# Eleven VectorE units in 21 of 28 pairs, vertical results in tiles of 128 tokens, and fewer groups of projections, in a cross-window attention kernel

## The chip, the cores and the metric

The kernel runs on one core of one Trainium2 chip. The metric is the device time of one launch in microseconds (us), as the median of several runs. The core has a matrix engine (TensorE, PE in the profile; its weight loads are PEld), a vector engine (VectorE, DVE), an activation engine (ScalarE, ACT), a general one (GpSimd, POOL) and a queue for transfers (SyncE, SP).

## The reference

The input x is an image of 224 x 224 tokens with 96 channels, in bf16. The first 48 channels of q, k and v attend within horizontal stripes of 8 rows, the other 48 within vertical stripes of 8 columns. Each stripe holds 8 x 224 = 1792 tokens, and there are 28 of each kind.

```
qkv = einsum('bhwc,cd->bhwd', x, wqkv)
q, k, v = qkv[..., :C], qkv[..., C:2*C], qkv[..., 2*C:]
# horizontal: 28 stripes of 8 rows, channels 0..47
ah = softmax(einsum('bqc,bkc->bqk', qh, kh) * scale)
oh = einsum('bqk,bkc->bqc', ah, vh)
# vertical: 28 stripes of 8 columns, channels 48..95
av = softmax(einsum('bqc,bkc->bqk', qv, kv) * scale)
ov = einsum('bqk,bkc->bqc', av, vv)
return einsum('bhwc,cd->bhwd', concat(oh, ov), wo)
```

## The kernel before

**Pairs, chunks, units.** Two stripes make a pair P; pairs 0 to 13 are horizontal, 14 to 27 vertical. A pair's 1792 queries are cut into four chunks (512, 512, 512 and 256). For a full chunk a *unit* is one tile of 128 keys against 512 queries of both stripes; for the last chunk it is two tiles of keys against 256 queries. Either way a unit is a score tile of 128 x 1024 in two banks of PSUM, and a pair has 14 + 14 + 14 + 7 = 49 units, 1372 in all. Scores (`qk_op`, line 985) split the array of TensorE by rows, one stripe in each half; the product with the values (`pv_op`, line 938) splits it by columns, one stripe in each half. The code calls these two shapes of the array modes "q" and "v", and its planner charges a constant for a change between them.

**Two ways to the exponential.** Most units go through ScalarE (`add_a`, line 1007): one ACTIVATE with Exp from PSUM to `PT`, then one product with the values. The others go through VectorE (`add_d`): line 1045 turns scores into integers `I_sb`, lines 1058 and 1060 split off mantissa and exponent (`U_sb`, `E_sb`) for two units at a time, line 1064 multiplies `I_sb` and `U_sb` to `G_sb` (halves on GpSimd, or a whole unit on VectorE), and both `E_sb` and `G_sb` are multiplied with the values. `NDC` and `NDP` say how many units of each chunk go this way: `[4, 2, 2, 2]`, and `[4, 3, 2, 2]` in seven pairs. An odd unit at a pair's end is processed alone.

**Projections** (`prep`) for pair P + 1 are done beside the units of P, as small groups called fills: one matmul group into a bank and a copy out of it. There are four for k (line 689, copy 706, then its mean is subtracted), four for q (copy 700) and four for v (line 745, copy 750: 10 and 4 tiles of keys for each stripe).

**Outputs** (`fin`). When a chunk's values are summed, VectorE copies them to `OT_sb` (line 901), and groups of four tiles are multiplied with `wo`. One more column holds the sum of the softmax: a reciprocal (lines 778, 831) and a product (797, 835) normalize. A horizontal pair has 7 groups. Its result goes to a staging buffer, and 8 DMAs on SP's queue carry it into `Ph_sb`, laid out by image rows for the vertical pairs. A vertical pair has 8 groups (two stripes, four chunks of four tiles of 112 rows of the image, each tile two matmuls), GpSimd adds the part from `Ph_sb` (line 839), and 8 DMAs store it.

**Order.** The order of the operations on TensorE, VectorE and GpSimd is written out by hand in `PLAN`: one digit an operation, naming the stream that gives the next one (in "pe": 1 scores for ScalarE, 2 scores for VectorE, 3 and 4 products with the values, 5 output groups, 6 fills). `far` says which products of line 1064 go to GpSimd, `bank` which banks are used. Each engine runs its list in order. A small planner with fixed costs puts in the waits and orders SP's queue.

Of the kernel before, what the change touches and what calls it, by code (L numbers as in the profile page):

```python
# [25 lines left out]
NDP = {P: [4, 3, 2, 2] for P in range(3, 28, 4)}  # L26


def ndc(P, c):
# [5 lines left out]
        "00000000000000000066611216162164144116444216331641631264144126133136121464441144441243141461643143124143614124"  # L35
        "31431241641241641144533123414312414531631313631531544163124154312414316341261341146444145145416414361331251341"
        "24163114644441335154124163124163412144414412414441214461431231631231331261343114443311464454114644531541641544"
        "14613313461231541241631145444413123614411634541246134125414414123134123134414412613312316412314313412641341164"
        "46411344336154154441512441636141253143144163153164412415341241431443121434124144146123613414414616312513331214"
        "44144126133113643441164454164154415416313312631441251341441146346134123164124135411444461231341234144124135414"  # L40
        "41461361335124163154144416312351441216341146444145144613313461231541241631145444413316451541231641231644124144"
        "14412414431251331134443513412514312416441231331461641136446411634441451441533126144123614411634411336445124315"
        "41146431246144124143314124513412415411346431641354123164124134163312414612314412414411346441231631134644415416"
        "51441431233134113664412313412413414412414312316441134463123614412613412413541331464154113446415416415441541633"
        "13612351441241631145444133615415441261341231641241444133124144123154411344361361241354124144144126133113634641"
        "14544341431231641241644116345441511344633154114634512461341412461421414313412415431245141134433164124163412614"
        "41231431346154143146414614124142133136114634541144461153331146445315412461312416441241441331241431241544113443"
        "35124154136124416312413314616441231361412133413514516441261431144443113644616431241544123143144125144412413311"
        "36344144615412415312513331241641231431341164463614611463441244154124143134616411534461441136433412514441136445"
        "12316414441241331241441231531441436136123154124134133124614311544441146446413312316441261341146445314416313514"  # L50
        "46135124153164144412614412414413341241541231541344121334124163124164411344631634113444614514361331251441241634"
        "11464431146335144411634515412341641241464124131312414411335441241641233163124153124144133126414311644644131213"
        "34114644541641231644111354444316313124416341126441341412641441233144112335144116344461312351441231634143163414"
        "12531341461444133161544126134412613411544441146335411463451244161235144124164411442313154123514411464431641241"
        "45312416412416431431451311363444314614514531431261443126144411643314531146435124316412414612414531144214331451"
        "43143146312416412414531241431431261334111644433441331216441126341441164463111644335411164435421451436121544121"
        "44142164111343335124414412613312316412316413341216441341134446124611133544163124614431154444113634515441631231"
        "54124414314412614412416431313531441461241644123133126134124613411444531631143444416451441541431631236134123164"
        "11454441163354124163124513412414414412641441133354123414144126313312614412316413314641154344114464451461544154"
        "16313312613412541341146444136135412416312413514412461441444123135123154113644412463341124316441251341431341144"  # L60
        "44164615431631331216441451363125144411144463341645135154124163124614412514441441213341231541134446312163415414"
        "41334163123164412613412415441431441631231641236144115443411343634164125414312414314416416331541541544131253143"
        "12441641261441412441331261441243134133114644641331445144124164124164114643631416331531231631251441231644115444"
        "41245142131331164434124164125133144126133143314641164443113463351451544146123164412513411464441146335414412513"
        "41241641241644114344412513312415311464431241631431261341241634115444411433344164164154415414615416331231531231"
        "64114644441451241331631241634115444412415413312415331241441541341534125144124133133154412415312415431215441441"
        "2541431341143443114335513413541541541241544124144133141431344554344355"),
    "dve": (
        "00000000000000000333333332332344323332344332323442331234421232344332123344333331332344323323443333331323323441"
        "33333232344221442323212444433333333333333132332344133233332344231244423123244232333443133333332334432333331234"  # L70
        "42324421344233312344232344333333333331232344331323234433221442331333323443333233234433331323323443133333323234"
        "42212443313323324423333333144333323234431333233323442123324413333332344233232244132444333333321443324422124431"
        "32323443233344333333333331323323441333333323234422124433133234423233334413323233334433133333323234421233244133"
        "32324423333443332213344333331333332323442212443133323332442333444212333333324433331234423233244441333323132332"
        "44233333331243423333334431233333234424214423313323442323443333312323344333331333233323442123324412332324433444"
        "33333132332344333313333323234424214433213232344232333441233333234434331234423234421233443132334443233432344133"
        "33232344331333333232332443123323344313233234443233344433333132323443133333232324431234443313232344232344413323"
        "23334431333332333234423213444233123234423244433321333323443433333331234423232344443133232123244333344433333431"
        "32323443133332323442323144423312323442333443333333333312323344133332342334423123323344321323444234443333333142"
        "33332344313333333323234423123234431323344433233232344133232344434331323442333443333313233231244232444233444331"  # L80
        "33232334433133232332344332312344321323344423334443333331333232334433313233232444312332334431232323344344433333"
        "4333333123323413434323234434321332344321333323444323323323132334432444434343133333333233442441443433133333"),
    "pool": (
        "00000000022222122222222222222222222212222222222222222222212222222222222222222212222222222222222222221222222222"
        "22222222221222222222222222222222212222222222222222221222222222222222222221222222222222222222222212222222222222"
        "22222122222222222222222222222122222222222222222221222222222222222222212222222222222222212222222233332222223222"
        "21222232233222222223221222233222233333222222333221222232222333322222222332212232222333223222232221222322333222"
        "23222222321222333222232233222232212222223322333322223223322122333222233332222223222122233322322222233333222221"
        "2222222333222222332212222332233333222222223312222333332232233223332222333333333333333"),
    "far": (  # L90
        "11111111111111111111111111110111111111111111111111111111111111111111111111111011111111111111111111111111111111"
        "11111011111111111111110111111111111011111101111110111110101111111001111110110111111011101110111110101111011111"
        "1101110101011110111100111101101111110101111011110110011001110000000"),
    "bank": (
        "76547012376502064256045260426403640246024604602472026027062705205205204620462042540520752057302570264026406204"
# [274 lines left out]
FUSED = 0.45  # L370
PRIO = (1, 0, 3, 5, 4, 2)
DPRIO = (0, 1, 2, 3)
HALVES = False
LEAD, SPACE, PACE, FIRST = 8, 3, 0.9, 0


# [817 lines left out]
```

## Time and profile before

| | |
|---|---|
| median of 3 runs | 1016.58 us (1015.27 to 1017.64) |
| profiled execution, its own time | 1017.69 us |
| its span, first to last instruction | 1015.6 us |
| mean granted TensorE clock | 0.995 |
| ScalarE busy | 1000.0 us (98%) |
| VectorE busy | 925.3 us (91%) |
| GpSimd busy | 695.1 us (68%) |

A line of instruction groups gives source line, engine, operation, what it writes and reads, shapes and count, then busy time in us, mean ns of one, and the idle time of that engine just before such instructions with what ended it. Instructions that overlap their neighbours have a mean longer than their step.

### The profile page before, as it was taken

The numbers are of one execution on the slowest core, as the hardware profiler recorded it, in microseconds if no ns is written. First come the engines' busy times: TensorE is split into PE (matmuls) and PEld (weight loads), VectorE is DVE, ScalarE is ACT, GpSimd is POOL, SyncE is SP. The second block draws the span as 40 slices with busy tenths as digits, with TensorE's granted clock in tenths as the row PEclk, the third lists the DMA queues.
The fourth block names the chain that finished last, engine by engine and source line by source line (L and its number), as shares of the span: only waits on it lengthen the run. The fifth ranks groups of instructions, "written<-read, shape, count | busy, mean of one in ns | idle before, by whom it ended". The sixth has DMA issues, their size and how long they took to land.

```text
span 1015.6 us, 25611 instructions
## 1 busy us (share of the span) xinstructions
PE 1001.6 (99%) x10683; PEld 388.2 (38%) x10683; DVE 925.3 (91%) x1677; ACT 1000.0 (98%) x1094; POOL 695.1 (68%) x639
## 2 busy tenths in 40 slices
PE   8999999999999999999999999999999999999998
PEld 3333333443334334334333333433343343334333
DVE  7999988998989988999899899989998999999998
ACT  6999999999999999999999999999999999999997
POOL 2777577667666756666677777776777676777674
PEclk8999999999999999999999999999999999999999
DMA  5121323353524425232442112212122221222112
GB/s 108 38 29 37 66 28 56 46 65 29 65 38 39 53 39 65 28 44 42 49 60 49 30 37 60 42 39 48 39 44 42 59 44 38 56 42 39 25 26 52
DMA packets 189612, 46.61 MB, mean 46 GB/s; under 512 B 189384, under 2 KB 189384, under 8 KB 189496
## 3 DMA queue, kind: packets, MB, share of 16 engines
q1 hardware_dynamic: 188536, 44.49, 27.2%
q8 instruction: 83, 1.36, 0.6%
q10 hardware_dynamic: 960, 0.49, 0.2%
q14 instruction: 33, 0.27, 0.1%
HBM read 0.44 MB, written 9.63 MB: 10 GB/s over the span
## 4 chain that ended last, share of the span: by engine, by line
ACT 74%; PE 23%; DVE 2%; POOL 1%; issue 0%; DVEq 0%
ACT PT L1007 74%; PE ps L938 10%; PE ps L985 9%; PE ps L689 2%; PE ps L826 1%; DVE I_sb L1045 1%; PE ps L745 1%; POOL G_sb L1064 0%; PE ps L529 0%; DVE OT_sb L901 0%; DVE E_sb L1060 0%; DVE tmp L835 0%; DVE QT_sb L700 0%; DVE U_sb L1058 0%; DVE V_sb L750 0%
## 5 line engine op out<-in xcount | busy, mean ns | idle before, releaser
L1007 ACT ACTIVATE PT<-ps 128x1024 bf16<-128x1024 f32 x1085 | 996.0, 1134 | 4.5 <-PE ps L985 4.4
L1064 POOL TENSOR_TENSOR G_sb<-I_sb,U_sb 128x512 bf16<-128x512 bf16 x488 | 549.5, 1155 | 285.1 <-DVE E_sb L1060 259.2
L985 PE MATMUL ps<-QT_sb,KT_sb 48*128 48x512 bf16 (+1 forms) x3136 | 469.7, 357 | 6.1 <-ACT PT L1007 3.2
L1045 DVE TENSOR_SCALAR I_sb<-ps 128x1024 int16<-128x1024 f32 x287 | 350.4, 1221 | 29.8 <-PE ps L985 25.6
L938 PE MATMUL ps<-PT,V_sb 128*64 128x512 bf16 (+1 forms) x2450 | 373.7, 364 | 0.0
L985 PEld LDWEIGHTS ps<-QT_sb,KT_sb 48*128 48x128 bf16 x3136 | 125.2, 93 | 311.0 <-ACT PT L1007 235.7
L938 PEld LDWEIGHTS ps<-PT,V_sb 128*64 128x64 bf16 x2450 | 120.2, 109 | 122.1 <-issue 101.8
L938 PE MATMUL ps<-G_sb,V_sb 128*64 128x512 bf16 (+1 forms) x686 | 111.6, 354 | 0.0
L839 POOL TENSOR_TENSOR out_sb<-tmp,Ph_sb 112x384 bf16<-112x384 f32 x111 | 99.0, 915 | 13.6 <-DVE G_sb L1064 5.3
L938 PE MATMUL ps<-E_sb,V_sb 128*64 128x512 bf16 (+1 forms) x686 | 101.3, 353 | 0.5 <-DVE OT_sb L901 0.2
L1058 DVE TENSOR_SCALAR U_sb<-I_sb 128x2048 int16<-128x2048 int16 x147 | 101.2, 689 | 0.0
L1060 DVE TENSOR_SCALAR E_sb<-I_sb 128x2048 int16<-128x2048 int16 x147 | 99.0, 674 | 0.0
L689 PE MATMUL ps<-xT_sb,w_sb 96*64 96x512 bf16 (+1 forms) x444 | 83.0, 369 | 0.7 <-ACT xT_sb L655 0.4
L700 DVE TENSOR_SCALAR QT_sb<-ps 128x512 bf16<-128x512 f32 (+1 forms) x111 | 68.4, 619 | 15.6 <-PE ps L689 12.5
L901 DVE CAST OT_sb<-ps 128x512 bf16<-128x512 f32 x112 | 69.3, 619 | 4.1 <-PE ps L938 3.2
L706 DVE TENSOR_SCALAR_CACHE_REDUCE KT_sb<-ps 128x512 bf16<-128x512 f32 x110 | 67.2, 620 | 5.5 <-PE ps L689 5.2
L750 DVE CAST V_sb<-ps 128x480 bf16<-128x480 f32 (+1 forms) x112 | 55.7, 502 | 12.2 <-PE ps L745 11.3
L835 DVE TENSOR_TENSOR tmp<-ps,rc 112x384 f32<-112x384 f32 x111 | 61.6, 555 | 2.7
L718 POOL TENSOR_SCALAR KT_sb<-KT_sb,negmean 128x1792 bf16<-128x1792 bf16 x27 | 47.5, 1761 | 18.4 <-DVE E_sb L1060 14.8
L797 DVE TENSOR_TENSOR out_sb<-ps,rc 128x384 bf16<-128x384 f32 x98 | 54.5, 556 | 2.8
L938 PEld LDWEIGHTS ps<-G_sb,V_sb 128*64 128x64 bf16 x686 | 34.9, 108 | 39.6 <-issue 28.4
L938 PEld LDWEIGHTS ps<-E_sb,V_sb 128*64 128x64 bf16 x686 | 31.1, 108 | 34.9 <-issue 19.0
(44 smaller groups left out, 339.3 us busy)
## 6 DMA issues: line engine op xcount, KB each, us to landing
Ph_sb<-out_sb SPq DMA_DIRECT2D x112, 84.0 KB, 4.3
out_dram<-out_sb SPq DMA_DIRECT2D x111, 84.0 KB, 2.0
xT_sb<-in_x_dram SPq DMA_TRANSPOSE x251, 2.5
Ph_sb<-in_x_dram ACTq DMA_DIRECT2D x1, 336.0 KB, 3.2
out_dram<-out_sb ACTq DMA_DIRECT2D x1, 84.0 KB, 2.2
wo_sb<-in_wo_dram SPq DMA_DIRECT2D x4, 9.0 KB
wo_sb<-one_sb SPq DMA_DIRECT2D x4, 0.0 KB
w_sb<-in_wqkv_dram ACTq DMA_DIRECT2D x1, 54.0 KB, 5.0
```

Of the source, the lines that this page charges most:

```text
L689: ins = e.matmul(bk[64 * w:64 * w + 64, 0:qs], lhsT=w_sb[0:C, wblk(P, kind), :], rhs=rhs, start=True, stop=True)
L700: return e.tensor_scalar(dst, src, A128, None, ALU.mult)
L706: return e.tensor_scalar(dst, src, 1.0, None, ALU.mult, ALU.add, accum_out=acc)
L839: return e.tensor_tensor(out_sb[b][0:HB, :, w, 2 * c:2 * c + 2, :].rearrange("p h d c -> p d h c"), tmp[hold[1].tok["t"]][0:HB, 0:n, :].re ...
L901: return e.tensor_copy(OT_sb[b][:, q0:q0 + qs], bk[:, 0:qs])
L938: return e.matmul(bank(k.bank)[64 * w:64 * w + 64, x0:x1], lhsT=lhs(w, kts[i])[p0:p1], rhs=rhs(w, i, qs)[p0:p1, x0:x1], start=(op.tok["fir ...
L985: ins = e.matmul(bank(op.tok["s"][w])[:, i * qs:(i + 1) * qs], lhsT=KT_sb[b][64 * w:64 * w + C2, kt * 128:(kt + 1) * 128], rhs=QT_sb[b][64 ...
L1007: a.fn = lambda e: e.activation(PT[a.tok["p"]][:].rearrange("p (s n) -> p s n", s=2), two(q.tok["s"]), ACTF.Exp, scale=LN128)
L1045: return e.tensor_scalar(dst[:, at:at + 1024].rearrange("p (s n) -> p s n", s=2), two(src), 128.0 * ONE, 0.0, ALU.add, ALU.max)
L1058: f.fn = lambda e: e.tensor_scalar(U_sb[y()][:, 0:m], I_sb[y()][:, 0:m], M_FRAC, HALF, ALU.bitwise_and, ALU.bitwise_or)
L1060: x2.fn = lambda e: e.tensor_scalar(E_sb[x2.tok["l"]][:, 0:m], I_sb[y()][:, 0:m], M_EXP, E_LOW, ALU.bitwise_and, ALU.bitwise_or)
L1064: g.fn = lambda e: e.tensor_tensor(G_sb[x2.tok["l"]][:, i0:i1], I_sb[y()][:, i0:i1].bitcast(BF16), U_sb[y()][:, i0:i1].bitcast(BF16), ALU. ...
```

## The change

Units on VectorE become 3, 3, 3 and 2 by chunk in the 21 pairs whose number isn't 1 modulo 4; the other seven keep 4, 2, 2 and 2. Queries of vertical pairs are put in the order (row, column in the stripe), so that a tile of 128 tokens is 16 image rows by 8 columns, as the horizontal results already have it. Horizontal results are therefore written straight to `Ph_sb`, and the staging DMAs go. A vertical pair has 7 output groups in place of 8; those of the three full chunks take one stripe each, in full tiles of 128 tokens with the contraction in one half of the array's rows (`rowed`, mode "q"), and the last chunk does both stripes in one group. Stores of a vertical pair become 16, all issued when its seventh group is added; the last pair stores tile by tile. The last fills of k and q share one bank, and v takes groups of 10, 10 and 8 tiles over both stripes: 10 fills in place of 12. All lists of `PLAN` are new.

```diff
-NDP = {P: [4, 3, 2, 2] for P in range(3, 28, 4)}
+NDP = {P: [3, 3, 3, 2] for P in range(28) if P % 4 != 1}
...
-        Ph_sb = sb("Ph_sb", [128, 2, 2 * NPH, SW, C], BF16)
-        out_sb = [sb(f"out_sb{i}", [128, 2, 2, SW, C], BF16) for i in range(2)]
+        Ph_sb = sb("Ph_sb", [128, NPH, WB, C], BF16)
+        out_sb = [sb(f"out_sb{i}", [128, NKT, 2, C], BF16) for i in range(2)]
...
-                        if kind == "q" and is_h[P]:
+                        if kind == "q":
                             rhs = xT_sb[b][0:C, w, :].rearrange("c (g t) -> c g t", g=SW)[:, :, q0 // SW:(q0 + qs) // SW]
...
+                        else:
+                            dst = dst.rearrange("p (t d) -> p t d", d=SW)
+                            src = src.rearrange("p (d t) -> p t d", d=SW)
...
+                if kind == "k" and c == NCH - 1 and not startup:
+                    pe_q, ev_q = kq("q", c, part=True)
+                    pe_k = pe_fn
+                    pe_fn = lambda e, bk: (pe_k(e, bk[:, 0:qs]), pe_q(e, bk[:, qs:2 * qs]))[1]
+                    evs.insert(1, ("dve", 0.08 + qs / 960, lambda e, bk, op: ev_q(e, bk[:, qs:2 * qs], op), [], True, dve_ev, [], None))
...
-            def vv(w, k0):
-                n = min(VS, NKT - k0)
+            def vv(k0, n=None):
+                n = n or min(VS, 2 * NKT - k0)
...
-                work = [(kq, kind, c) for kind in "kq" for c in range(NCH)] + [(vv, w, k0) for w in range(2) for k0 in range(0, NKT, VS)]
+                work = [(kq, kind, c) for kind in "kq" for c in range(NCH - (kind == "q"))] + [(vv, k0) for k0 in range(0, 2 * NKT, VS)]
...
-                        return e.tensor_tensor(stage(b)[:, g[0]:g[0] + n, :], ...
+                        return e.tensor_tensor(Ph_sb[:, P, g[0]:g[0] + n, :], ...
...
-                            fn = lambda e, dw=dw: e.dma_start(Ph_sb[r0:r0 + 2 * SW, P // 7, :, dw, :], stage(b)[dw:128:8, :, :])
...
+                for ws in ((0,), (1,)) if nk == 4 else ((0, 1),):
+                    n = nk * len(ws)
+                    last = P == NP - 1 and c == NCH - 1
+                    rowed = VQ and len(ws) == 1
...
+                            if rowed:
+                                ins = e.matmul(bk3[:, s, :], lhsT=OT_sb[b][64 * w:64 * w + CA, t0:t0 + 128], rhs=wo_sb[1][w][64 * w:64 * w + CA, :],
+                                               start=True, stop=True)
+                                continue
+                            for p0 in (0, 64):
+                                ins = e.matmul(bk3[p0:p0 + 64, s, :], lhsT=OT_sb[b][:, t0 + p0:t0 + p0 + 64], rhs=wo_sb[1][w][:, :], start=True, stop=True)
...
+                        elif len(added[P]) == 7:
+                            for d in range(SW):
+                                for w in range(2):
+                                    dst = bass.AP(out.tensor, out.offset + (SW * (j0 + w) + d) * C, [[W * C, 16], [16 * W * C, NKT], [1, C]])
+                                    parts.append((dst, out_sb[b][d:128:SW, :, w, :], added[P]))
...
+                    if rowed:
+                        p.mode = "q"
...
-                prep(P + 1, pace=lambda n, base=base: [act_of[base + int(n * NA * PACE / 12)]])
+                prep(P + 1, pace=lambda n, base=base: [act_of[base + int(n * NA * PACE / 10)]])
```

More of the change, by code (lines that the diff above doesn't have):

```diff
@@ L373 @@
 HALVES = False
+VQ = True
 LEAD, SPACE, PACE, FIRST = 8, 3, 0.9, 0
@@ L885, in fin @@
                     fin_pe[P].append(p)
-        def evs_of(P, c):
-            return [chunks[(P, i)].evac for i in range(max(0, c - 1), c + 1)]
+        added = {P: [] for P in range(NP)}
         def pv_done(k, op):
```

288 lines of the change are left out of this document (138 added, 150 removed).

## The prediction

> **What bounds the kernel now.** I read the page first (shares of the engines, the chain that ended last), then the stages, then the chain in order of time, then single steps in the timeline.
>
> ```profile
> span 1015.6 us, 25611 instructions
> PE 1001.6 (99%) x10683; PEld 388.2 (38%) x10683; DVE 925.3 (91%) x1677; ACT 1000.0 (98%) x1094; POOL 695.1 (68%) x639
> ACT 74%; PE 23%; DVE 2%; POOL 1%; issue 0%; DVEq 0%
> L1007 ACT ACTIVATE PT<-ps 128x1024 bf16<-128x1024 f32 x1085 | 996.0, 1134 | 4.5 <-PE ps L985 4.4
> ```
>
> ScalarE does 1085 exponentials and sits idle 4.5 us in front of them. TensorE is nearly as full, though its ends are modelled, so 99% alone proves little; the chain says more: three quarters of it is ScalarE, a quarter is TensorE. So two engines bind in turns, and VectorE is third. The stages of the second half (columns: PE, PEld, DVE, ACT, POOL busy, then clock, DMA share, GB/s) show how far VectorE can be filled:
>
> ```profile
> 700.00:800.00 100.00, 99.34 (x1096) 38.67 (x1092) 92.24 (x169) 99.55 (x109) 74.01 (x69) 1.00 0.22 45
> 800.00:900.00 100.00, 99.41 (x1062) 37.60 (x1062) 93.89 (x172) 99.89 (x110) 70.94 (x67) 1.00 0.22 45
> 900.00:1000.00 100.00, 99.49 (x1086) 38.89 (x1085) 95.17 (x175) 99.93 (x110) 68.55 (x67) 1.00 0.16 33
> sum 500.00, PE 495.87 PEld 191.71 DVE 464.90 ACT 499.37 POOL 354.66; mean PE 99.17 PEld 38.34 DVE 92.98 ACT 99.87 POOL 70.93
> ```
>
> With VectorE 95.17% busy ScalarE still ran 110 instructions in 100 us without a gap. DMA is busy a fifth of the time. What one exponential costs, one behind the other, stands in the chain:
>
> ```profile
> 30.08 639.29 ACT PT L1007 x697
> 913.06 76.20 ACT PT L1007 x83
> ```
>
> 639.29 / 697 = 0.917 us and 76.20 / 83 = 0.918 us; the 1134 ns of the group are longer because neighbours overlap.
>
> **Part 1: fourteen units leave ScalarE.** The old counts are 10 units in 21 pairs and 11 in 7 (287), the new ones 11 in 21 and 10 in 7 (301); the digits "2" in the two TensorE orders count the same. So 1085 exponentials become 1071: 14 x 0.917 = **-12.8 us** of ScalarE. That is the whole gain if ScalarE alone sets the end.
>
> **Part 2: TensorE.** Its steps, from start to start:
>
> ```profile
> 301.31 0.62 PE L938 MATMUL ps<-PT,V_sb 128*64 128x512 bf16 x4
> 301.87 0.60 PE L985 MATMUL ps<-QT_sb,KT_sb 48*128 48x512 bf16 x4
> 302.43 0.41 PE L689 MATMUL ps<-xT_sb,w_sb 96*64 96x512 bf16 x2
> 302.77 0.39 PE L985 MATMUL ps<-QT_sb,KT_sb 48*128 48x512 bf16 x2
> 303.09 0.41 PE L938 MATMUL ps<-G_sb,V_sb 128*64 128x512 bf16 x2
> 303.33 0.38 PE L938 MATMUL ps<-PT,V_sb 128*64 128x512 bf16 x2
> ...
> 501.14 0.36 PE L790 MATMUL ps<-wo_sb,OT_sb 128*64 128x97 bf16 x8
> 501.30 0.11 PEld L938 LDWEIGHTS ps<-G_sb,V_sb 128*64 128x64 bf16 x2
> 501.34 0.38 PE L938 MATMUL ps<-G_sb,V_sb 128*64 128x512 bf16 x2
> ```
>
> Between two operations of the same shape of array (303.09 to 303.33, both column-split) a 512-column operation takes 0.24 us. From row-split scores to column-split values (302.77 to 303.09) it takes 0.32, from a projection to scores (302.43 to 302.77) 0.34. So a change of shape costs 0.08 to 0.10 us; I take 0.09. The steps hold no wait that one could take away: TensorE is really full here.
>
> Counting the changes of shape along the two written orders, with six of seven vertical output groups counted as row-split in the new one, gives 1888 before and 1814 after: 74 x 0.09 = **-6.7 us** (5.9 to 7.4). A unit on VectorE is multiplied with the values twice (E and G), one on ScalarE once: 14 more steps of 0.24, **+3.4 us**. Vertical output groups fall from 8 to 7 a pair, 14 in all, at 0.20 us each (501.14 to 501.34 for eight matmuls): **-2.8 us**. Projections keep their columns; fuller groups save only changes of shape, which are counted. New are 84 row-split output groups of four matmuls of 97 columns with weights of 128 columns. No row shows one. The nearest is the 256-column score operation, where two loads of 128 columns fall to each row half:
>
> ```profile
> 507.23 0.11 PEld L985 LDWEIGHTS ps<-QT_sb,KT_sb 48*128 48x128 bf16 x4 [0.41 <-ACT PT L1007]
> 507.23 0.39 PE L985 MATMUL ps<-QT_sb,KT_sb 48*128 48x256 bf16 x4
> ...
> L985 PEld LDWEIGHTS ps<-QT_sb,KT_sb 48*128 48x128 bf16 x3136 | 125.2, 93 | 311.0 <-ACT PT L1007 235.7 <-issue 16.7 <-DVE I_sb L1045 13.0
> ```
>
> All four loads are over in 0.11 us, so two in one half need at most 0.055 each: a group takes at most 0.22 us. The least is its stream: the eight matmuls above ran as four pairs in at most 0.20, so 0.05 a pair, and 97 columns at the pace of 512 in 0.24 are 0.045, or 0.18. Against the 0.20 of today that is -1.7 to +1.7 over 84 groups; I take 0. TensorE: -6.7 + 3.4 - 2.8 = **-6.1 us**, bounds -3.6 and -8.5.
>
> **Part 3: VectorE.** Rows, by form:
>
> ```profile
> L1045 DVE TENSOR_SCALAR I_sb<-ps 128x1024 int16<-128x1024 f32 x287 | 350.4, 1221 | 29.8 <-PE ps L985 25.6
> L835 DVE TENSOR_TENSOR tmp<-ps,rc 112x384 f32<-112x384 f32 x111 | 61.6, 555 | 2.7
> L750 DVE CAST V_sb<-ps 128x480 bf16<-128x480 f32 x56 | 36.5, 653 | 7.6 <-PE ps L745 7.2
> L1064 DVE TENSOR_TENSOR G_sb<-I_sb,U_sb 128x1024 bf16<-128x1024 bf16 x43 | 29.7, 694 | 0.0
> L831 DVE RECIPROCAL rc<-ps 112x4 f32<-112x4 f32 x112 | 19.9, 177 | 4.5 <-PE ps L826 3.6
> L750 DVE CAST V_sb<-ps 128x192 bf16<-128x192 f32 x56 | 19.6, 352 | 4.5 <-PE ps L745 4.1
> L1058 DVE TENSOR_SCALAR U_sb<-I_sb 128x1024 int16<-128x1024 int16 x7 | 3.2, 459 | 0.0
> L1060 DVE TENSOR_SCALAR E_sb<-I_sb 128x1024 int16<-128x1024 int16 x7 | 2.9, 418 | 0.0
> ```
>
> The five pairs of units of each P stay; the eleventh stands alone, so 14 more single units: 14 x 1.221 = +17.1 and 14 x (0.459 + 0.418) = +12.3. The list of placements holds 56 products on VectorE where there were 43: 13 x 0.694 = +9.0. Fourteen vertical groups go: 14 x (0.555 + 0.177) = -10.2. The value copies of a pair go from two of 480 and two of 192 columns (2.01 us) to two of 480 and one of 384, which by the line through the two rows is 0.55 (1.86): 27 x 0.15 = -4.1. Sum **+24.1**, so 949.4 us, 94.4% of a span of 1006. That lies under the 95.17% of the stage 900 to 1000, so I charge the path only 1.0 us for it (0 to 4.5, the latter if every 100 us lose the 0.45 by which the worst 100 us here, 700 to 800, fell short).
>
> The query copies of vertical pairs change from a straight copy to one that reads PSUM with a step of 64 elements. The rows nearest are those of today's copies, horizontal ones (permuted in runs of eight) in the first window, straight ones in the second:
>
> ```profile
> 14.00:497.00 483.00, 35.61 (x58) 0.99 0.34 46
> 497.00:1016.00 519.00, 32.10 (x52) 1.00 0.22 43
> ...
> L700 DVE TENSOR_SCALAR QT_sb<-ps 128x512 bf16<-128x512 f32 x83 | 57.0, 687 | 9.7 <-PE ps L689 8.2 <-PE ps L682 0.2
> L700 DVE TENSOR_SCALAR QT_sb<-ps 128x256 bf16<-128x256 f32 x28 | 11.7, 419 | 5.9 <-PE ps L689 4.3 <-PE ps L682 1.6
> ```
>
> 35.61 / 58 = 0.614 and 32.10 / 52 = 0.617 us: the permutation costs nothing, and I take 0. The other bound, every column at twice the time, is the third rival. A gain isn't possible, the straight copy being the least there is.
>
> **Part 4: GpSimd, DMA, tail.** GpSimd loses 14 additions and gains 2 products; it was busy 695 us and is no bound. The 112 staging transfers go, and with them the wait of the horizontal products for a free staging buffer. Stores become 16 a vertical pair in pieces of one token (192 bytes) instead of 8 in pieces of two, all issued when the seventh group of the pair is added, on SP's queue ahead of the next loads of x. Those loads are for two pairs ahead; a pair lasts about 1015.6 / 28 = 36 us, and that covers the burst, so nothing. Without the cover the first projections of the pair would wait for the burst. At the very end two vertical groups become one:
>
> ```profile
> 1011.25 0.56 DVE L835 TENSOR_TENSOR tmp<-ps,rc 112x384 f32<-112x384 f32 x1
> 1011.72 0.17 DVE L831 RECIPROCAL rc<-ps 112x4 f32<-112x4 f32 x1
> ```
>
> That takes at most 0.7 us out of the tail; four stores on two queues give some back. I take -0.4 (-0.7 to +0.6).
>
> **The sum.** ScalarE's load falls by 12.8, TensorE's by 6.1, and the chain ran 74% over the one and 23% over the other. An estimate that weighs them so: 0.74 x 12.8 + 0.23 x 6.1 = 10.9. With +1.0 and -0.4 it is -10.3 us. The profiled execution took 1017.69 us (2.1 outside the span), so 1007.4; it lay 1.1 above the median of 1016.58, so **1006.3**. Alternating binds as today: 1003 to 1010.
>
> **The rivals.** *TensorE becomes the only bound.* For it: TensorE loses half of what ScalarE loses, so it is now the fuller one; against it, part of its waits today are for ScalarE. Then 3.6 to 6.1 us arrive, from 1016.6: 1010.5 to 1013.
>
> *ScalarE alone sets the end, and its small gaps shrink too*, since TensorE waits less on shape changes. All 12.8 arrive and up to 3 more: 1000.5 to 1003.
>
> *VectorE becomes the bound in the second half, slower.* If the strided read doubles the time of a column, (687 - 419) / 256 = 1.05 ns, the 14 vertical pairs pay 14 x (3 x 0.536 + 0.268) = 26 us. From 500 to 1000 us VectorE had 464.9; half of the new units, all of the vertical savings give +7; with 26 it is 498. At 95.2%, the fullest stage seen, that takes 523 us: 23 more than now, 5 less in the first half, so about 1034. It decides from some 10 us of extra VectorE time, 0.2 us a copy. Against it speak the 0.614 and 0.617. The Trainium skill, SBUF — State Buffer, section on the DMA port swizzle, says that PSUM has lines of 8 bytes, that an access crossing to a new line pays, and that patterns that aren't contiguous slow matmuls down. By that rule the new copies, each element 256 bytes from the last, pay and the result is this rival; the permuted rows here, 32 bytes in a run, agree with neither side of it.
>
> *The weights of the row-split groups aren't hidden, slower.* If each of 336 matmuls took load and stream, the 93 ns of the row of such loads and 45 of stream, instead of 50, TensorE would get 336 x 0.088 = 30 us: -6.1 + 30 gives 1040. The Trainium skill, TensorE: Matmul & The Clock Gate, part 3, "The mechanism", says that a load overlaps running matmuls only where the row group differs; these four share one, and its section on LDWEIGHTS prices 128 columns at 107 ns, which would make it some 1045. The row of four loads in 0.11 us, two to a row group, speaks against it.
>
> *The new written order simply idles more*: engines run in order, and every list is new; a wait of 0.05 us in one of five units costs 14 us: about 1020. And *it may come to nothing* (within 0.2%). That the units don't move is excluded by the counts.
>
> **How the numbers follow.** Forecast 0.52, TensorE alone 0.15, ScalarE alone 0.13: these three hold 0.80 and reach from 1000.5 to 1013; with the tail's and the copies' bounds 1000 to 1014.5. VectorE slower 0.08, weights 0.03, order 0.05, nothing 0.04. So faster 0.80, same 0.04, slower 0.16; 0.2% is 2 us, about the spread of the three times before (1015.27 to 1017.64).
>
> **What would show it.** 1071 exponentials at 0.915 to 0.92 each; idle in front of them under 10 us; a chain with more TensorE than 23%; VectorE near 949 us; vertical query copies still 0.68 us; row-split groups at 0.2 us from start to start. It is wrong if the step of the exponentials rises over 0.928 (then the 14 are given back), if vertical query copies take over 0.9 us, or if a row-split group takes over 0.3.

## The result, and the profile after

The kernel after the change takes 1009.77 us (median of 4 runs, 1008.67 to 1011.48), beside 1016.52 us for the kernel before on the same chip. The ratio is 0.9943, with a 95% interval of 0.9929 to 0.9957. The forecast was 1006.3 us, in a range of 1000.0 to 1014.5. Of the 12.8 us that leave ScalarE, a bit over half arrives.

The page of the profile after (its own time 1011.48 us) begins:

```profile
span 1009.7 us, 24732 instructions
PE 992.5 (98%) x10263; PEld 387.3 (38%) x10263; DVE 941.9 (93%) x1677; ACT 988.6 (98%) x1080; POOL 685.3 (68%) x627
ACT 61%; PE 33%; SPq 3%; DVE 2%; issue 0%; DMA 0%; DVEq 0%
L1017 ACT ACTIVATE PT<-ps 128x1024 bf16<-128x1024 f32 x1071 | 984.5, 1122 | 8.9 <-PE ps L995 7.4
```

ScalarE is busy 11.4 us less, but its idle time ahead of the exponentials doubled, from 4.5 to 8.9 us, and 7.4 us of it waits for scores. The chain has less of ScalarE and more of TensorE than the 74% and 23% before. The chain in order of time shows where (start, length, line and count; the longest pieces on ScalarE):

```profile
53.34 53.30 ACT PT L1017 x58
...
186.61 124.95 ACT PT L1017 x136
312.54 145.91 ACT PT L1017 x159
...
853.17 77.20 ACT PT L1017 x84
```

145.91 / 159 = 0.918 us: an exponential that follows another costs what it did. But the longest stretch in the chain is 159 exponentials where it was 697. So the loss stands between the stretches, in single long steps. From the start of every exponential in the two traces:

| steps of ScalarE, start to start | before | after |
|---|---|---|
| exponentials | 1085 | 1071 |
| mean step | 0.9212 us | 0.9266 us |
| shortest steps | 0.904 us | 0.904 us |
| lost over 0.904 in steps above 1.1 us | 5.1 us | 12.7 us |
| lost in steps of 0.96 to 1.1 us | 7.5 us | 6.2 us |
| lost in steps below 0.96 us | 6.1 us | 5.3 us |
| last exponential's end to the span's end | 6.2 us | 7.3 us |

The account of the span: 14 steps fewer, 14 x 0.9212 = -12.9; 1070 steps longer by 0.0054 each, +5.8; tail +1.0; start +0.1; together -6.0, and the spans differ by 5.9. The account names one thing to explain: twelve new steps of 1.3 to 1.7 us, and one of 2.33. Beside the few at the start, before had two (1.62 us at 28.5 us of the span, 1.73 at 798.4).

The start hides a part of the loss. TensorE's granted clock was 0.5 there for 3.4 us in this execution and for 6.8 us in that of before, and the first twelve steps took 12.7 us and 14.3 us (11.2 in executions without such a stretch, as that of `after_thin_dve` below). From the 13th exponential on, the mean step rose from 0.9182 to 0.9251 us: 1058 x 0.0069 = 7.3 us.

**What such a stop looks like.** The timeline of the kernel after around one of them (start, length, engine, line, what; in brackets the idle time before it and what ended it):

```profile
146.74 3.90 ACT L1017 ACTIVATE PT<-ps 128x1024 bf16<-128x1024 f32 x4
...
149.77 0.36 PE L801 MATMUL ps<-wo_sb,OT_sb 128*64 128x97 bf16 x8
149.93 0.37 PEld L948 LDWEIGHTS ps<-PT,V_sb 128*64 128x64 bf16 x6
149.97 0.81 PE L948 MATMUL ps<-PT,V_sb 128*64 128x512 bf16 x6
...
150.71 0.48 PEld L995 LDWEIGHTS ps<-QT_sb,KT_sb 48*128 48x128 bf16 x10 [0.41 <-ACT PT L1017]
150.72 0.83 PE L995 MATMUL ps<-QT_sb,KT_sb 48*128 48x256 bf16 x10
151.15 1.02 ACT L1017 ACTIVATE PT<-ps 128x1024 bf16<-128x1024 f32 x1 [0.51 <-PE ps L995]
```

The fourth exponential ends at 146.74 + 3.90 = 150.64. Only then, at 150.71, do the scores of the next unit start, and the next exponential starts 0.44 us after them. Reading the written lists "pe" and "bank" tells why: these two units for ScalarE, one right after the other, were given the *same* pair of PSUM banks, so the scores must wait until the exponential has emptied it. Mostly two pairs alternate. In the lists of before this happens at 2 places, and they are its two long steps; in the lists of after at 5 (units 37, 149, 187, 878 and 1015). At such a moment most of the other banks are held: by the sums of chunks, by a unit for VectorE, by fills and output groups. At two more places in after, units 43 and 1023, the next unit shares one of its two banks with the unit before it, and waits in the same way.

At four places (after units 681, 756, 811 and 909) the next exponential has its scores and waits for a place to write. `PT` has eight buffers, and by the written order the product that reads the one needed, eight units back, comes two or three operations behind the scores in TensorE's list. The exponential that follows unit 811:

```profile
761.61 0.81 PE L948 MATMUL ps<-PT,V_sb 128*64 128x512 bf16 x6
762.03 1.94 ACT L1017 ACTIVATE PT<-ps 128x1024 bf16<-128x1024 f32 x2 [0.50 <-PE ps L948]
```

The last two kinds are scores that stand late in TensorE's list (unit 583) and scores behind something that waits (unit 731). The step at unit 1023, and what unit 731 waits for:

```profile
956.45 2.00 ACT L1017 ACTIVATE PT<-ps 128x1024 bf16<-128x1024 f32 x2
...
957.77 0.68 DVE L911 CAST OT_sb<-ps 128x512 bf16<-128x512 f32 x1
...
958.56 0.12 PEld L995 LDWEIGHTS ps<-QT_sb,KT_sb 48*128 48x128 bf16 x2 [0.23 <-DVE OT_sb L911]
...
685.81 0.41 PE L683 MATMUL ps<-xT_sb,w_sb 96*64 96x512 bf16 x2 [1.02 <-DMA xT_sb<-in_x_dram]
```

In the first, one bank of the scores held the sum of a chunk and the other belonged to the exponential just before. The copy of the sum and that exponential both end at 958.45 (957.77 + 0.68 and 956.45 + 2.00), so either alone would have held the scores as long, and ScalarE starts again about 0.55 later. The second is the step of 2.33 us: a projection waits 1.02 us for a load of x, and the scores stand behind it. SyncE's queue shows what the load was behind:

```profile
639.40 11.29 SPq L876 DMA_DIRECT2D out_dram<-out_sb  x16
650.79 13.32 SPq L555 DMA_TRANSPOSE xT_sb<-in_x_dram  x10
664.15 11.50 SPq L876 DMA_DIRECT2D out_dram<-out_sb  x16
675.70 15.20 SPq L555 DMA_TRANSPOSE xT_sb<-in_x_dram  x11
```

The queue never rests from 639 to 691 us: 16 stores take 11.3 us of it, and they come in bursts ahead of the loads.

Added up over 0.904 us a step, the seven places with a shared bank are 5.2 us (the two of before 1.5), the four that wait for `PT` 2.2, unit 583 0.7 and unit 731 1.4. That is 8.0 us more than before, and the shorter steps win 0.7 back.

### The profile page after: what moved, and what is told of

It reads as the page before. It is cut to its first block, busy times and chain, and to the rows that moved or that the text cites. A ratio compares the mean times of both kernels' runs of the same rounds, so it can differ in the third digit from the quotient of the medians.

```text
span 1009.7 us, 24732 instructions
## 1 busy us (share of the span) xinstructions
PE 992.5 (98%) x10263; PEld 387.3 (38%) x10263; DVE 941.9 (93%) x1677; ACT 988.6 (98%) x1080; POOL 685.3 (68%) x627
## 4 chain that ended last, share of the span: by engine, by line
ACT 61%; PE 33%; SPq 3%; DVE 2%; issue 0%; DMA 0%; DVEq 0%
ACT PT L1017 60%; PE ps L948 15%; PE ps L995 13%; PE ps L683 2%; SPq L555 2%; PE ps L754 1%; SPq L876 1%; DVE I_sb L1055 1%; PE ps L801 1%; PE ps L831 0%; PE ps L529 0%; DMA xT_sb<-in_x_dram 0%; DVE KT_sb L703 0%; DVE G_sb L1074 0%; PE ps L835 0%
## 5 line engine op out<-in xcount | busy, mean ns | idle before, releaser
L1017 ACT ACTIVATE PT<-ps 128x1024 bf16<-128x1024 f32 x1071 | 984.5, 1122 | 8.9 <-PE ps L995 7.4
L1055 DVE TENSOR_SCALAR I_sb<-ps 128x1024 int16<-128x1024 f32 x301 | 367.2, 1220 | 24.5 <-PE ps L995 19.9
L948 PE MATMUL ps<-E_sb,V_sb 128*64 128x512 bf16 (+1 forms) x714 | 109.5, 355 | 0.5 <-DVE E_sb L1070 0.3
L1068 DVE TENSOR_SCALAR U_sb<-I_sb 128x2048 int16<-128x2048 int16 (+1 forms) x161 | 105.8, 657 | 0.1
L1070 DVE TENSOR_SCALAR E_sb<-I_sb 128x2048 int16<-128x2048 int16 (+1 forms) x161 | 104.9, 652 | 0.0
L847 POOL TENSOR_TENSOR out_sb<-tmp,Ph_sb 128x384 bf16<-128x384 f32 x84 | 75.1, 912 | 25.6 <-DVE U_sb L1068 7.6
L683 PE MATMUL ps<-xT_sb,w_sb 96*64 96x512 bf16 (+1 forms) x444 | 78.0, 367 | 2.5 <-DMA xT_sb<-in_x_dram 1.0
L808 DVE TENSOR_TENSOR Ph_sb<-ps,rc 128x384 bf16<-128x384 f32 x98 | 54.5, 556 | 2.8
L841 DVE TENSOR_TENSOR tmp<-ps,rc 128x384 f32<-128x384 f32 x97 | 53.9, 555 | 2.8 <-POOL out_sb L848 0.4
L759 DVE CAST V_sb<-ps 128x480 bf16<-128x480 f32 (+2 forms) x85 | 51.7, 610 | 1.1 <-PE ps L754 0.6
```

Source lines behind the costliest of these rows:

```text
L683: ins = e.matmul(bk[64 * w:64 * w + 64, 0:qs], lhsT=w_sb[0:C, wblk(P, kind), :], rhs=rhs, start=True, stop=True)
L847: return e.tensor_tensor(out_sb[b][:, k0:k0 + nk, ws[0], :], t, Ph_sb[:, k0:k0 + nk, j0 + ws[0], :], ALU.add)
L948: return e.matmul(bank(k.bank)[64 * w:64 * w + 64, x0:x1], lhsT=lhs(w, kts[i])[p0:p1], rhs=rhs(w, i, qs)[p0:p1, x0:x1], start=(op.tok["fir ...
L1017: a.fn = lambda e: e.activation(PT[a.tok["p"]][:].rearrange("p (s n) -> p s n", s=2), two(q.tok["s"]), ACTF.Exp, scale=LN128)
L1055: return e.tensor_scalar(dst[:, at:at + 1024].rearrange("p (s n) -> p s n", s=2), two(src), 128.0 * ONE, 0.0, ALU.add, ALU.max)
L1068: f.fn = lambda e: e.tensor_scalar(U_sb[y()][:, 0:m], I_sb[y()][:, 0:m], M_FRAC, HALF, ALU.bitwise_and, ALU.bitwise_or)
```

## The experiments

**Theory T**: TensorE sets the end (33% of the chain), and its 6 us are what arrived. **Theory V**: VectorE, fuller by 17 us, frees banks late. **Theory S**: the written order itself: stops at fixed places, in which engines wait for each other once around, whatever each engine's load.

### TensorE's load, up and down

In `vv`, the matmuls of the first half of each fill's tiles are issued twice:

```diff
-                    for j in range(n):
+                    for j in [*range(n), *range(0 if startup else n // 2)]:
```

> The changed kernel with more work on TensorE alone: in each of the 27 preparations the first half of every value-projection group's matmuls is issued a second time into the same place (14 of 28 tiles, 0.033 us each from the row of the groups of 10 tiles, so 27 x 14 x 0.033 = 12.5 us; no other engine gets anything). Theory T (TensorE's sequence sets the end, ScalarE lies close behind): 9 to 13 us longer than the changed kernel, about 1020. Rival W (the two bind by the shares of the chain, TensorE 33%): 4 us, 1014. Rival V (VectorE, fuller by 17 us, sets the end): under 3 us.

> The kernel before with the same 12.5 us more on TensorE (14 of 28 tiles of value projections in each of 27 preparations issued twice). Theory T: 7 to 12 us longer, since TensorE's sequence sets the end there too but ScalarE is nearly level: about 1026. Rival W (chain share 23%): 3 us, 1019.5. Rival V: under 2 us.

In the other direction, the product of `E_sb` with the values runs on a quarter of its columns, in both kernels:

```diff
+                n = qs // 4 if thin and not op.tok["first"] and k.last is not op else qs
...
-                        ins = mm(e, i, w, 0, 0, qs, 0, 128)
+                        ins = mm(e, i, w, 0, 0, n, 0, 128)
```

> The changed kernel with less work on TensorE: the product of E_sb with the values takes a quarter of the columns (unless it is the first or last of its chunk), so the output lacks that part; 301 units lose up to 0.16 us, some 45 us in all. VectorE, GpSimd and ScalarE keep all of theirs. Theory T: the end falls until ScalarE alone sets it, 1071 steps of 0.905 to 0.91 and about 21 us ahead and behind: 991 to 998. Rival V (VectorE and GpSimd at their limit): falls by less than 4 us, over 1005.

> The kernel before with the same cut (product of E_sb with the values on a quarter of the columns; 287 units). Theory T: 1085 steps of 0.905 to 0.91: 1003 to 1010, and 11 to 14 us above the changed kernel with the same cut, so the 12.8 us of ScalarE that did not arrive would stand there. Rival V: falls by less than 4 us, and the difference between the two stays near 7.

| | time | ratio to before | 95% interval |
|---|---|---|---|
| after, more TensorE | 1017.88 us | 1.0022 | 1.0010 to 1.0035 |
| before, more TensorE | 1021.98 us | 1.0071 | 1.0054 to 1.0087 |
| after, thin E products | 1010.75 us | 0.9956 | 0.9941 to 0.9971 |
| before, thin E products | 1014.5 us | 0.9998 | 0.9985 to 1.0011 |

The kernel before was timed anew beside each set of runs: 1014.8 us here, 1016.18 and 1016.37 us in the two sets below. The kernel after itself has the ratio 0.9943.

The page of the kernel after with the thin products:

```profile
PE 977.8 (97%) x10263; PEld 384.3 (38%) x10263; DVE 942.3 (93%) x1677; ACT 988.6 (98%) x1080; POOL 685.2 (68%) x627
ACT 86%; PE 12%; DVE 1%; issue 0%; DVEq 0%
L1018 ACT ACTIVATE PT<-ps 128x1024 bf16<-128x1024 f32 x1071 | 984.6, 1153 | 8.3 <-PE ps L996 7.3
```

TensorE left the chain, from 33% to 12%, and nothing was gained: the idle time in front of the exponentials is still 8.3 us, and the long steps stand at the same units with the same lengths within 0.15 us at most of them (unit 811 is 0.32 shorter, the late load of unit 731 costs 1.1 less). TensorE's busy time fell by 14.7 us, less than the 45 expected, but its idle time ahead of scores rose from 6.6 to 20.4 us: it waits more, and ScalarE no less. So Theory T, which wanted 991 to 998 us, falls. In before, the same thinning puts ScalarE at 96% of the chain with 3.0 us idle, and again the time stays: before was bound by ScalarE's own steps.

The load added tells another thing. 12.5 us of matmuls (by the estimate) cost 8 us in after (0.0079 of 1015) and 7 us in before. Taken alone that lies nearest to Theory T (9 to 13 us and 7 to 12 us); it is the load taken away that speaks against it. The two are best read together, though no run shows this reading by itself: TensorE has no room to give, although it isn't what sets the end, since in-order work ahead of scores delays them, while work taken away leaves them waiting for the same bank.

### VectorE's load, up and down

An extra copy of 384 columns out of PSUM in one of the fills of each pair (27 of 0.55 us):

```diff
+                    if n == 8:
+                        e.tensor_copy(spare[b][:, 0:n * C2], bk[:, 0:n * C2])
```

> The changed kernel with one more copy of 384 columns from PSUM to a spare buffer on VectorE beside the third value copy of each of 27 preparations: 27 x 0.55 = 14.9 us on VectorE alone. Theory V (VectorE, 93% busy, holds ScalarE up): 10 to 15 us longer, 1020 to 1025. Theory S (the loss lies at some fourteen fixed places of the written order, where the next scores for ScalarE come a whole round trip late, because their banks are still held by the exponential before or because they stand late): 1 to 6 us, 1011 to 1016.

And `U_sb` and `E_sb` of pairs of units computed for half of their columns (`cut(m, ...)` gives 1024 in place of 2048; the other half keeps older values):

```diff
-            f.fn = lambda e: e.tensor_scalar(U_sb[y()][:, 0:m], I_sb[y()][:, 0:m], M_FRAC, ...
+            f.fn = lambda e: e.tensor_scalar(U_sb[y()][:, 0:cut(m, "u", y())], I_sb[y()][:, 0:cut(m, "u", y(), True)], M_FRAC, ...
```

> The changed kernel with less work on VectorE: U_sb and E_sb are made for half of the columns of a pair of units (after each buffer's first full use; the output is off by that), 270 instructions shorter by 0.27 us, some 70 us less on VectorE and less blocking of GpSimd. Theory V: ScalarE runs at its own step of 0.917 all through and all 12.8 us arrive: 1001 to 1004. Theory S: stops at the banks of the exponential before it stay (5 of them), only those behind VectorE go: 1005 to 1009.

> The kernel before with the same cut on VectorE (U_sb and E_sb for half of the columns). Both theories: ScalarE has nearly no stop here, so 0 to 3 us less: 1013 to 1016.

| | time | ratio to before | 95% interval |
|---|---|---|---|
| after, more VectorE | 1017.14 us | 1.0007 | 0.9996 to 1.0019 |
| after, thin VectorE | 1009.83 us | 0.9938 | 0.9922 to 0.9955 |
| before, thin VectorE | 1016.02 us | 0.9996 | 0.9984 to 1.0008 |

```profile
PE 990.8 (98%) x10263; PEld 384.9 (38%) x10263; DVE 878.4 (87%) x1677; ACT 988.4 (98%) x1080; POOL 685.6 (68%) x627
ACT 63%; PE 35%; DVE 1%; issue 0%; DVEq 0%
L1017 ACT ACTIVATE PT<-ps 128x1024 bf16<-128x1024 f32 x1071 | 984.3, 1120 | 6.6 <-PE ps L995 5.1
```

In the thin kernel VectorE is at 87%, below what it was in before, and the gain can't be told from nothing. Theory V falls in the same way. (The idle time of 6.6 us instead of 8.9 is the start, where this execution had no stretch at a clock of 0.5, and the step at the late load of x, here 1.29 us; every other long step has the length of after within 0.01 us.) Theory S was wrong too in one point: it had the steps behind VectorE go, and they stayed. Again the load added costs: 14.9 us give about 6.5 us (0.0064 of 1016), just over the 1 to 6 of Theory S, and nine further long steps appear.

Both reliefs at once:

> Both reliefs at once on the new kernel: the product of E_sb with the values on a quarter of its columns (some 45 us less for TensorE) and U_sb and E_sb of pairs for half of their columns (some 70 us less for VectorE); that part of the output is left out. Theory S (the stops are places of the written order and of its bank list, which stay): the ratio stays within 0.006 of the 0.9943 of the new kernel, about 1007 to 1011 us, and steps of ScalarE over 1.3 us stay at the units 149, 187, 583, 811, 878, 909, 1015 and 1023. Rival R (TensorE and VectorE relieve each other, so that neither thinning alone could show): the long steps go and ScalarE runs at the 0.917 of before, 1071 x 0.917 against 1071 x 0.9266 now, so some 10 us less, about 999 to 1001.

Measured: 1010.59 us, ratio 0.9938 (0.9924 to 0.9953). Its page:

```profile
PE 977.1 (97%) x10263; PEld 381.8 (38%) x10263; DVE 878.6 (87%) x1677; ACT 988.5 (98%) x1080; POOL 686.2 (68%) x627
L1018 ACT ACTIVATE PT<-ps 128x1024 bf16<-128x1024 f32 x1071 | 984.5, 1151 | 8.5 <-PE ps L996 7.6
```

With both engines unloaded, ScalarE still idles 8.5 us, 7.6 of it for scores, at the same units. Rival R, 999 to 1001 us, falls too.

### The stops alone

The straight test of Theory S puts stops into the kernel *before*, with no work added and the orders of all engines as they were: ten digits of the list of banks are changed, so that at ten more places two successive units for ScalarE share a pair of banks.

```diff
-        "30623036503603062350632063063206320614360136520653062506035620362046206013613613641262461241602462641264162145"
+        "30623036503603062350632063063206320614360136520653062506035620362046206013613613641262461241602462641224162145"
```

> The kernel before with ten digits of the list of banks changed, so that at ten places two units that follow each other on ScalarE use the same pair of banks (two such places before, five in the changed kernel). No work is added. Theory S: each such step takes 1.6 to 1.7 us in place of 0.92, and what is lost there is not made up: 6 to 8 us longer, 1021 to 1024. If such stops are caught up later, or the two bounds are TensorE or VectorE: under 2 us.

Measured: 1025.69 us, ratio 1.0094 (1.0077 to 1.0111), so +9.5 us, 0.95 us a place, where 6 to 8 us in all were expected. The first of the ten in the timeline, and the same stretch of before:

```profile
67.37 2.06 ACT L1007 ACTIVATE PT<-ps 128x1024 bf16<-128x1024 f32 x2
...
69.48 0.61 PE L985 MATMUL ps<-QT_sb,KT_sb 48*128 48x512 bf16 x4 [0.76 <-ACT PT L1007]
...
69.91 1.94 ACT L1007 ACTIVATE PT<-ps 128x1024 bf16<-128x1024 f32 x2 [0.49 <-PE ps L985]
```

```profile
67.57 3.87 ACT L1007 ACTIVATE PT<-ps 128x1024 bf16<-128x1024 f32 x4
```

With the added stop two exponentials take 69.91 - 67.37 = 2.54 us from start to the next start; in before four in a row follow each other without idle time. The ten steps measured 1.56 to 1.83 us, as the five in after (1.57 to 1.71), and are 0.74 us longer each than the same steps in before. The rest of the 0.95 us comes behind them. The longest step of this execution, 2.33 us, is none of the ten: it stands two units behind the ninth, where TensorE had been idle for 1.33 us and its granted clock was then 0.50 for 3.4 us (the third number from the end of the second line):

```profile
691.34 1.03 PE L985 MATMUL ps<-QT_sb,KT_sb 48*128 48x256 bf16 x8 [1.33 <-ACT PT L1007]
...
693.00:694.00 1.00, 1.00 (x12) 0.86 (x10) 0.00 (x0) 0.93 (x2) 1.00 (x1) 0.50 0.50 102
```

That step alone is 1.4 us over the usual. Whether the idle time brought the lower clock isn't tested.

So the price of such a place is shown, 0.74 us by itself and 0.95 with what followed here. After has seven such places, with the two that share one bank, and before had two: 5.2 - 1.5 = 3.7 us by their own steps, 5 x 0.95 = 4.8 us by this price, of the 7.3 us lost from the 13th exponential on. That is a half or somewhat more. The rest lies in the long steps of the other kinds shown above. Their places stay under every relief of load too, but no run here took them out, so their cause is read from the lists and the trace alone. A written order without the new stops wasn't run; at the mean step of before it would, as an estimate, end 7.3 us earlier, at about 1002.5 us.

### Two parts of the change

One part undone: the vertical output groups column-split as before.

```diff
-VQ = True
+VQ = False
```

> One part of the change undone: the 84 vertical output groups of full chunks are column-split (eight matmuls with weights of 64 columns) in place of row-split (four with 128). Nothing else differs, the order of the lists stays. The prediction put both groups at about 0.20 us, and the shape of array beside them decides the rest: a group that stood between two score operations now makes two changes of shape of 0.09 more. Theory S (TensorE's few tenths lie off the path): 0 to +2 us. Rival T (TensorE is on the path with most of its load): up to 84 x 0.18 = 15 us more for TensorE, and by the 8 us that 12.5 us of extra matmuls cost, +5 to +10 us. A gain of over 2 us would show that the loads of the row-split groups are not hidden.

Measured: 1013.83 us, ratio 0.9974 (0.9961 to 0.9986), 3.1 us slower than after, between the two expectations; neither number was right. TensorE's busy time rises by 3.7 us, from 992.5 to 996.2 (2.7 of them from the 13th exponential on), not by 15: most groups change shape on one side already (64 of 84 stand between scores and a product with the values). And a part of the time is two new long steps near the end, 1.47 and 1.74 us at units 1010 and 1011, where after has 0.90 and 0.97. So the row-split form is worth 3 us, and its loads are hidden.

And half of the stores of vertical pairs left out:

```diff
-                            for d in range(SW):
+                            for d in range(0, SW, 2):
```

> Every other store of the vertical pairs but the last left out (8 in place of 16 a pair, so half of those results are not stored), the rest as it is. The prediction put nothing for the stores. If they delay loads of x only now and then (1 us once in the profiled execution): 0 to -1.5 us against the new kernel. If the burst is a lasting cost of the change, by holding up transfers and so first projections in each of 13 pairs: -5 us or more.

Measured: 1009.09 us, ratio 0.9931 (0.9915 to 0.9948), which isn't distinguishable from after. The step that was 2.33 us is 1.26 here, and every other long step is as it was; but with all the stores it was 1.26 and 1.29 in the profiles of the two kernels with one load thinned, 1.44 in that with both, and 2.38 with column-split groups. So the late load of x comes in some executions and then costs about 1 us; whether the stores cause it, the runs don't settle. A lasting cost of the burst is excluded.

## Why the prediction was right or wrong

**ScalarE's 14 units: right.** 1071 exponentials, and 0.917 each where nothing interrupts them (145.91 / 159 = 0.918). All 12.8 us left ScalarE's list.

**The combination: the step that failed.** 0.74 x 12.8 + 0.23 x 6.1 weighed two loads by their shares of the chain. The runs show that neither share is a price: with the thin products TensorE's share fell from 33% to 12% and its busy time by 14.7 us for nothing, and in before its share fell from 23% to 4% for nothing. A chain over two engines that take turns can be followed on either at the same instant. What counts is ScalarE's load plus its waits, and the waits are set by the order. The sum then is -12.9 + 5.8 + 1.0, where the prediction had, in effect, -10.9 + 1.0 - 0.4. (Of the 5.8, +7.3 is the order and -1.6 the start.) That the time still lies in the range is in part luck: the gain from the two loads was taken 2 us too small, and the stops of the new order, which the sum holds no term for, took more than that back. Its sign of failure, a step over 0.928, was nearly reached: 0.9266, and the 0.915 to 0.92 that it expected was missed. Idle time under 10 us was right, at 8.9, but only part of a long step counts there as idle.

**The rival "the written order simply idles more" had the mechanism and was given 0.05.** It was priced as 0.05 us in one of five units, 14 us. It came as twelve long steps of 0.4 to 0.8 us over 0.904 and one of 1.4, which hold 8.0 us more than the two of before. Its places could have been read before the run: the bank list says where two successive units share a bank, and before showed what that costs, with its steps of 1.62 and 1.73 us.

**TensorE: the size about right, the weight wrong.** Busy time fell by 9.1 us, 7.7 of it from the 13th exponential on, where -6.1 was forecast (-3.6 to -8.5). The row-split groups by form, and the loads in front of them:

```profile
L831 PE MATMUL ps<-wo_sb,OT_sb 49*128 49x97 bf16 x336 | 27.6, 203 | 0.0
L831 PEld LDWEIGHTS ps<-wo_sb,OT_sb 49*128 49x128 bf16 x336 | 22.1, 94 | 11.8 <-DVE OT_sb L911 1.1 <-DVE KT_sb L703 0.7 <-DVE QT_sb L697 0.6
```

From the start of such a group to the next operation it takes 0.22 us without a change of shape and 0.27 with one (medians); the forecast was 0.18 to 0.22. 336 matmuls never waited (0.0 idle). The rival of exposed loads needed 0.093 + 0.045 a matmul, 0.55 a group, and is out. The Trainium skill, TensorE: Matmul & The Clock Gate, part 3, "The mechanism", would have had it that way by its line that a load overlaps running matmuls only where the row group differs, since all four loads of a group go to one row group; this trace disagrees with that line, with 94 ns a load and 0.22 us for four loads and four matmuls. It fits the first paragraph of the same section, which also lets a load go ahead into a background weight buffer.

**VectorE: mis-sized, 16.6 us in place of 24.1, and no bound.** By form:

```profile
L1055 DVE TENSOR_SCALAR I_sb<-ps 128x1024 int16<-128x1024 f32 x301 | 367.2, 1220 | 24.5 <-PE ps L995 19.9
L1068 DVE TENSOR_SCALAR U_sb<-I_sb 128x1024 int16<-128x1024 int16 x21 | 8.8, 419 | 0.0
L1070 DVE TENSOR_SCALAR E_sb<-I_sb 128x1024 int16<-128x1024 int16 x21 | 8.8, 420 | 0.0
L841 DVE TENSOR_TENSOR tmp<-ps,rc 128x384 f32<-128x384 f32 x97 | 53.9, 555 | 2.8 <-POOL out_sb L848 0.4
L1074 DVE TENSOR_TENSOR G_sb<-I_sb,U_sb 128x1024 bf16<-128x1024 bf16 x56 | 37.9, 684 | 0.1
```

The counts are those of the prediction, and the groups add up to about 20 us more than before. The engine's busy time rose by less since neighbours overlap: a mean of one instruction counts time that the next one also counts, as the prediction had said of the exponentials and then forgot for VectorE. The charge for it, 1.0 us (0 to 4.5), has no measured counterpart: unloading VectorE by 64 us gains nothing.

**The strided query copies: right, at nothing.**

```profile
L697 DVE TENSOR_SCALAR QT_sb<-ps 128x512 bf16<-128x512 f32 x83 | 56.5, 685 | 5.4 <-PE ps L683 4.9
L697 DVE TENSOR_SCALAR QT_sb<-ps 128x256 bf16<-128x256 f32 x28 | 11.8, 422 | 1.7 <-PE ps L676 0.9
```

685 and 422 ns beside 687 and 419 before, although half of them now read elements 256 bytes apart (128 in the copies of 256 columns). The vertical pairs alone have 684 and 421 ns, and 686 and 417 before. The Trainium skill, SBUF — State Buffer, section on the DMA port swizzle, with its lines of 8 bytes in PSUM, spoke for slower copies, though its sentence on patterns that aren't contiguous names matmuls alone; for VectorE's reads of f32 this case doesn't show it. The rival at 1034 us is out.

**Stores, "nothing": right as a steady cost**, with the reserve that the 36 us of a pair were not as empty as assumed: the queue was busy throughout from 639 to 691, and a load of x came 1.02 us late in the profiled execution.

**The tail: wrong in sign, +1.0 for -0.4 (-0.7 to +0.6).** The vertical group that goes does save what was said: from the last copy of a sum to the last `out_sb` operation it is 1.11 us where it was 1.79. The end behind that is 0.5 us longer, with four stores. And in the new order the last unit for VectorE comes later: its product `G_sb` starts after the end of the last exponential (1003.12 against 1002.40) where before it started ahead of it (1008.91 against 1009.42), and the last copy, output group and stores hang on it. That copy starts 1.9 us after the last exponential where it was 0.7.

```profile
1003.12 0.69 DVE L1074 TENSOR_TENSOR G_sb<-I_sb,U_sb 128x1024 bf16<-128x1024 bf16 x1
...
1004.31 0.43 DVE L911 CAST OT_sb<-ps 128x256 bf16<-128x256 f32 x1 [0.51 <-PE ps L948]
...
1005.42 0.99 DVE L855 SCALAR_TENSOR_TENSOR out_sb<-ps,rc,Ph_sb 128x96 bf16<-128x96 f32 x4
```

**A slip in a rival's bounds.** ScalarE alone with all 12.8 us and up to 3 more gives 1016.6 - 12.8 = 1003.8 and 1000.8, not 1003 and 1000.5; nothing hangs on it.

**What stays open**: whether the long steps can be ordered away within eight banks and eight buffers of `PT`, what makes one load of x late in some executions only, and when the granted clock drops.

## What to carry to other kernels

When engines run written orders, a unit taken off the fullest engine brings its full step, and then the new order gives some back: look for the places where the next unit's input must wait for the last one's output (the same buffer, or one bank of it, twice in a row, or a buffer whose reader stands later in the list), and price each as a full round trip. A share of the chain of waits is where one chain ran, not what a load there is worth; test it by making that load smaller, because making it larger costs time even where making it smaller gains none.

## What the hardware showed that was not expected

Two successive units in the same pair of PSUM banks cost 0.74 us each by themselves, and 0.95 with what followed in the run with ten: matmul, exponential and matmul come one behind the other, 1.6 to 1.8 us in place of 0.92. One shared bank costs as much (1.60 us at unit 43). The first twelve exponentials take 11.2, 12.7 or 14.0 to 14.3 us, as TensorE's granted clock is 0.5 there for 0, 3.4 or 6.8 us, which differs from execution to execution. Four loads of 128 columns into one row half, each for its own matmul of 97 columns, run at 0.22 us together, so they hide behind each other though they share the rows. And VectorE reads f32 from PSUM with steps of 256 bytes as fast as in sequence (685 and 687 ns for 512 columns).
